# Block attention with a mixture of experts on one core: when the first weight parts are loaded and split

## Chip, core and metric

One NeuronCore of a Trainium2 chip runs the kernel; a core has five engines that run side by side, each its own list of instructions in order: TensorE (PE in the profile, its weight loads PEld), VectorE (DVE), ScalarE (ACT), GpSimd (POOL) and SyncE (SP), which here issues nearly all DMAs. The metric is the device time in microseconds (us), the median of several runs. Lower is better.

## What is computed

Attention over 4 batches, 8 heads, 576 positions and a head size of 64, where a position sees its own 64-block and all earlier ones; its output, laid out as a [2304, 512] matrix `x`, goes through four experts with weights `p`:

```python
attn = softmax(mask(q @ k.T / 8))          # mask: block_i >= block_j, blocks of 64
x = (attn @ v) as [B*S, H*D]               # [2304, 512]
p = domain_probs / (domain_probs.sum(-1, keepdims=True) + 1e-9)
for e in range(4):
    h = np.maximum(x @ w1[e], 0.0)         # [2304, 1024]
    out += p[:, e:e + 1] * (h @ w2[e])     # [2304, 512]
```

All is float32. A float32 product in the experts is made as three products of a fast format (`fp32r`): each operand is split into a high part (a CAST) and a low part (operand minus high part, a TENSOR_TENSOR), and high x high, low x high and high x low are added.

## The kernel before

**Blocks and chunks.** The 2304 rows of `x` are cut into five blocks (`BLOCKS`): the first has 256 rows, the first 64 positions of each batch, the other four 512 rows each. The experts' work on a block is cut into 32 chunks, (expert, 128 of the 1024 hidden columns). Chunk i has two steps on PE: `mm1` (L1009), 12 matmuls `h <- w1h/w1l, xh/xl` in four groups of three, one group for each quarter of the 512 columns of `x`; and `mm2` (L1051), `acc <- w2h/w2l, hh/hl`, three matmuls for each 128 rows of the block (two such tiles in the first block). Between them `relu` (L1037) makes `hh` on ACT and `hl` on DVE. `moe_thread` (L996) runs mm1(0), mm1(1), mm2(0), mm1(2), mm2(1) and so on.

**Weights.** Two threads, `w_thread(1)` for W1 and `w_thread(2)` for W2 (L945), go through the chunks. `w_load` (L938) takes one of three raw buffers (`w1r0` to `w1r2`, `w2r0` to `w2r2`) and issues a 256 KB DMA; `w_split` (L971) then has `halves` (L961) make the high part (CAST on ACT or DVE) and the low part (on DVE) into one of four buffers `w1h0` to `w1h3`, `w1l0` to `w1l3`, and the same for W2, and gives the raw buffer back.

**The first block's attention** (`first_block`, L801) runs before everything else, in four steps of two heads (`step`, L824; step c0 makes quarter c0 of `x`). A step transposes K and Q on PE (L840), multiplies them (L864), takes the row maximum on DVE (L879, L881), exponentials on ACT (L884), the division on DVE (L888 to L890, result in `o3`), transposes the result (L894, copied to `xs` on ACT), multiplies with V (L907), and splits the result into `xh` and `xl`. `left_first[0]` counts the steps that are still open: it is 4 at first and 0 when the last `xl` of the first block is recorded. While PE would be idle in this stage, `warm_up` (L364) puts in matmuls whose result nobody reads (L365).

**The attention of the other blocks** is cut into 16 units (`unit`, L390), each a batch and two heads; the K, Q and V of a unit are loaded into `kr`, `qr` and `VN` (L402, L436, L463), transposed on DVE into `kT` (L416) and `qT` (L450) once `left_first[0]` is 0, and multiplied on PE (L510 in the first four units). PE mixes this with the experts' work on blocks that are ready.

**What sets the order.** A recording layer (`Flow`, L77) runs all threads when the program is built. Each thread offers its next operation; the layer estimates when each could start, takes the earliest, and at equal times the lowest priority number (L182 to L185). So each engine's list of instructions is fixed when the kernel is built, and a thread that says `("until", condition)` offers nothing until the condition holds in the recording. `w_prio` (L934) gives the priority of a weight part's DMA and splits: as long as chunk 0 is current (`now[0] == 0`) it is 1.6 for chunk 0 and 2.005 for all later ones; the first unit's K and Q have 2.0, its V 2.005 (L470), the first block's loads 1.1 and its steps 1.2 to 1.23.

Of the kernel before, what the change touches and what calls it, by code (L numbers as in the profile page):

```python
# [211 lines left out]
def kernel(  # L212
# [131 lines left out]
    def a_copy(dst, src, n, r, u, prio=0.0, ps=False):  # L344
        engs = [("act", 0.833 * n + (55 if ps else 95)), ("dve", (1.04 if ps else 0.52) * n + 70)]
        o = op(engs, 0, lambda e: nc.scalar.copy(dst, src) if e == "act" else nc.vector.tensor_copy(dst, src), r, u, prio)  # L346
        o.port = not ps
        return o

    def tt(eng, dst, a, b, alu, n, r, u, prio=0.0):  # L350
        both = {"dve": 1.04 * n + 70, "pool": 2.1 * n + 365}
        engs = [(e, both[e]) for e in (eng if isinstance(eng, list) else [eng])]
        o = op(engs, 0, lambda e: ENG[e].tensor_tensor(out=dst, in0=a, in1=b, op=alu), r, u, prio)  # L353
        o.port = a.space != PSUM and b.space != PSUM
        return o
# [24 lines left out]
    now, loads = [0], [0]  # L380
    left_first = [len(STEPS)]
# [551 lines left out]

    def w_prio(i, which):  # L934
        i -= 4 * (i >= NC) * (which == 1)
        return lambda: (1.6 if i == 0 else 2.005) if now[0] == 0 else 1.0 if i <= now[0] + 1 else (2.5 if i <= now[0] + 2 else 5.0)

    def w_load(which, i, e, f):  # L938
        raw = yield fl.take(f"w{which}r")
# [18 lines left out]
    def flat(raw):  # L958
        return raw.tile.rearrange("p c f -> p (c f)") if len(raw.tile.shape) == 3 else raw.tile

    def halves(which, turn, src, n, deps, raw, pr, more=()):  # L961

        hi = yield fl.take(f"w{which}h", turn)
        lo = yield fl.take(f"w{which}l", turn)
        a = yield a_copy(hi.tile[:, :n], src, n, deps, [raw, hi], pr)
        o = tt(BOTH, lo.tile[:, :n], src, hi.tile[:, :n], SUB, n, deps + [a], [raw, hi, lo], pr)
        o.pen = lambda: 1000.0 if now[0] == 0 else 300.0
        l = yield o
        return hi, lo, a, l

    def w_split(which, i, raw, v0, pr):  # L971
        wt[i, which] = yield from halves(which, i, flat(raw), DM, [v0], raw, pr)
        fl.give(raw)

# [429 lines left out]
```

## Time and profile before

| | |
|---|---|
| median of 3 runs | 898.09 us (897.37 to 898.21) |
| the profiled execution's own time | 898.77 us |
| span of its trace, first to last instruction | 896.7 us |
| PE busy | 887.7 us, 99% of the span |
| DVE, ACT, POOL busy | 689.0, 455.7, 139.4 us |
| HBM read and written | 85.63 MB and 4.72 MB |

The trace is of one execution. 2.1 us of its 898.77 lie outside the span. An engine counts as busy while an instruction of it runs; ends of matmuls are modelled, so a busy PE is not a PE at its peak. The granted clock is the share of TensorE's full clock (2.4 GHz) that it was given; 0.50 is 1.2 GHz.

### The profile page before, as it was taken

To read this page: it belongs to the slowest core of one execution; us is meant where nothing else is said; L and a number is where in the kernel's file an instruction comes from. 1 tells how busy PE (TensorE), PEld (TensorE's weight loads), DVE (VectorE), ACT (ScalarE), POOL (GpSimd) and SP (SyncE) were. 2 spreads that over 40 slices of the span, in tenths; PEclk is the share of its full clock that TensorE was granted. 3 is DMA by queue.
4 is the path that set the end of the run, shared out by engine and by line. 5 is a ranking of instruction groups with operands and counts; after the bars stand their busy time and mean duration, and the time that the engine had idled before them with its cause. 6 is when DMAs were issued, how large, how long until landed. Compare 5 with 4: busy or idle time off the path is not lost.

```text
span 896.7 us, 12489 instructions
## 1 busy us (share of the span) xinstructions
PE 887.7 (99%) x4342; PEld 715.7 (80%) x4344; DVE 689.0 (77%) x1293; ACT 455.7 (51%) x886; POOL 139.4 (16%) x53
## 2 busy tenths in 40 slices
PE   8999999999999999999999999999999999999998
PEld 5677788877787887787787787888888888888886
DVE  6799998989888988997897787975565655666532
ACT  4687765656556556665555554655343333333220
POOL 1111000244312232414213413000000000000000
PEclk9999999999999999999999999999999999999999
DMA  7775547724553554454443233312120212110002
GB/s 173 187 205 153 160 130 183 202 84 110 122 145 73 127 122 120 144 133 110 112 114 96 74 104 96 127 60 60 36 71 30 77 36 71 47 48 24 12 1 94
DMA packets 212734, 91.17 MB, mean 102 GB/s; under 512 B 126400, under 2 KB 193984, under 8 KB 212672
## 3 DMA queue, kind: packets, MB, share of 16 engines
q1 hardware_dynamic: 210464, 89.59, 37.5%
q10 hardware_dynamic: 2208, 0.79, 0.4%
q8 instruction: 34, 0.56, 0.3%
q14 instruction: 28, 0.23, 0.1%
HBM read 85.63 MB, written 4.72 MB: 101 GB/s over the span
## 4 chain that ended last, share of the span: by engine, by line
PE 95%; DMA 2%; DVE 1%; ACT 1%; issue 0%; SPq 0%; DVEq 0%; ACTq 0%
PE h L1023 24%; PE acc L1074 24%; PE acc L1310 19%; PE h L1247 10%; PE att L1247 7%; PE att L734 5%; PE att L522 2%; PE att L523 2%; DMA w2r<-in_moe_w_dram 1%; PE acc L510 1%; DMA cm<-in_q_dram 1%; PE att L510 0%; PE acc L734 0%; SPq L340 0%; ACT o L884 0%
## 5 line engine op out<-in xcount | busy, mean ns | idle before, releaser
L1023 PE MATMUL h<-xl,w1h 128*128 128x512 f32 (+1 forms) x384 | 136.3, 355 | 2.0 <-DVE xl L353 1.8
L1023 PE MATMUL h<-xh,w1h 128*128 128x512 f32 (+1 forms) x384 | 137.7, 359 | 0.0
L1023 PE MATMUL h<-xh,w1l 128*128 128x512 f32 (+1 forms) x384 | 136.2, 355 | 0.0
L1074 PE MATMUL acc<-w2h,hh 128*128 128x512 f32 x312 | 123.4, 395 | 0.0
L1074 PE MATMUL acc<-w2l,hh 128*128 128x512 f32 x312 | 121.8, 390 | 0.0
L1074 PE MATMUL acc<-w2h,hl 128*128 128x512 f32 x312 | 121.6, 390 | 0.0
L346 ACT CAST w2h<-w2r 128x512 fp32r<-128x512 f32 x113 | 70.5, 623 | 71.1 <-PE acc L1074 56.3
L667 POOL PARTITION_ALL_REDUCE sb<-sa x24 | 78.4, 3315 | 137.5 <-DVE sa L353 92.3
L688 POOL PARTITION_ALL_REDUCE mx<-cm x16 | 56.9, 3554 | 268.1 <-DVE cm L353 211.6
L353 DVE TENSOR_TENSOR w1l<-w1r,w1h 128x512 fp32r<-128x512 f32 (+1 forms) x124 | 85.9, 693 | 0.6
L353 DVE TENSOR_TENSOR w2l<-w2r,w2h 128x512 fp32r<-128x512 f32 x116 | 80.6, 697 | 7.0 <-ACT w2h L346 6.7
L1041 ACT ACTIVATE hh<-h 128x512 fp32r<-128x512 f32 (+1 forms) x94 | 49.4, 526 | 67.2 <-PE h L1023 66.3
L1023 PEld LDWEIGHTS h<-xl,w1h 128*128 128x128 f32 x384 | 72.8, 190 | 12.6 <-DVE xl L353 2.4
L1023 PEld LDWEIGHTS h<-xh,w1h 128*128 128x128 f32 x384 | 72.7, 189 | 12.1 <-issue 1.7
L1023 PEld LDWEIGHTS h<-xh,w1l 128*128 128x128 f32 x384 | 72.7, 189 | 10.3
L346 ACT CAST w1h<-w1r 128x512 fp32r<-128x512 f32 x116 | 69.1, 598 | 14.2 <-PE att L1247 5.7
L1074 PEld LDWEIGHTS acc<-w2h,hh 128*128 128x128 f32 x312 | 58.8, 188 | 12.9 <-issue 2.1
L1074 PEld LDWEIGHTS acc<-w2h,hl 128*128 128x128 f32 x312 | 58.6, 188 | 12.8
L346 ACT COPY S<-att 128x512 f32<-128x512 f32 (+2 forms) x92 | 49.0, 532 | 36.5 <-DVE att L592 21.6
L1074 PEld LDWEIGHTS acc<-w2l,hh 128*128 128x128 f32 x312 | 58.8, 188 | 10.2
L353 DVE TENSOR_TENSOR S<-S,mx 128x1024 f32<-128x1024 f32 (+4 forms) x80 | 60.2, 789 | 3.2 <-POOL mx L688 3.2
L1043 DVE SCALAR_TENSOR_TENSOR hl<-h,hh 128x512 fp32r<-128x512 f32 (+1 forms) x94 | 55.2, 587 | 6.3 <-ACT hh L1041 6.0
(336 smaller groups left out, 1812.8 us busy)
## 6 DMA issues: line engine op xcount, KB each, us to landing
w2r<-in_moe_w_dram SPq DMA_DIRECT2D x128, 256.0 KB, 2.9
w1r<-in_moe_w_dram SPq DMA_DIRECT2D x120, 256.0 KB, 3.0
qr<-in_q_dram SPq DMA_DIRECT2D x112, 64.0 KB, 2.3
kr<-in_k_dram SPq DMA_DIRECT2D x64, 72.0 KB, 2.9
VN<-in_v_dram SPq DMA_DIRECT2D x32, 128.0 KB, 2.5
out_dram<-o SPq DMA_DIRECT2D x12, 256.0 KB, 2.1
w1rp<-in_moe_w_dram SPq DMA_DIRECT2D x8, 256.0 KB, 2.9
out_dram<-op SPq DMA_DIRECT2D x4, 256.0 KB, 2.1
```

Of the source, the lines that this page charges most:

```text
L346: o = op(engs, 0, lambda e: nc.scalar.copy(dst, src) if e == "act" else nc.vector.tensor_copy(dst, src), r, u, prio)
L353: o = op(engs, 0, lambda e: ENG[e].tensor_tensor(out=dst, in0=a, in1=b, op=alu), r, u, prio)
L522: nc.tensor.matmul(out=o, lhsT=KK.tile[:, at:at + n], rhs=Hv[:, hs, lo:W], start=True, stop=False)
L667: sums.append((yield op("pool", 150 + 6.3 * W, lambda _, h=h: nc.gpsimd.partition_all_reduce(sb.tile[:, h * W:h * W + W], sa.tile[:, h * W ...
L688: lambda _: nc.gpsimd.partition_all_reduce(mx.tile[:, :2 * W], src, P, RED.max),
L734: nc.tensor.matmul(out=x.tile[64 * g:64 * g + 64, W - w:W], lhsT=lhsT, rhs=rhs, start=(i == 0), stop=(i == len(todo) - 1))
L1023: nc.tensor.matmul(out=ps[:, :n], lhsT=s.tile[:, ks], rhs=x.tile[:, kc, :n], start=(kc == 0 and m == 0), stop=(kc == KC - 1 and m == 2),)
L1041: a = yield op("act", 0.833 * n + 55, lambda _: nc.scalar.activation(hh.tile[:, :n], ps[:, :n], AF.Relu), [mm], [pb, hh], 0.0)
L1043: l = yield op("dve", 1.04 * n + 70, lambda _: nc.vector.scalar_tensor_tensor(out=hl.tile[:, :n], in0=ps[:, :n], scalar=0.0, in1=hh.tile[: ...
L1074: nc.tensor.matmul(out=acc, lhsT=s.tile[:, ts], rhs=w.tile, start=(f == 0 and m == 0), stop=(f == FC - 1 and m == 2))
L1247: nc.tensor.matmul(out=ps[:, :n], lhsT=w.tile[:, ks], rhs=x[:, kc, :n], start=(start and kc == 0 and m == 0), stop=(i in (2, 3, 4) and kc ...
L1310: nc.tensor.matmul(out=acc, lhsT=s.tile[:, ts], rhs=w.tile, start=(c == 0 and x == 0), stop=(c == 3 and x == 2))
```

## The change

Two edits. The priority of the W1 part of chunk 1 (`i + which == 2` holds for i = 1 and which = 1 alone, since chunk 0 is named before) goes from 2.005 to 1.7 while chunk 0 is current, so that its DMA is recorded ahead of the first unit's K, Q and V. And every other weight part after chunk 0's two (`i + which > 2`: W2 of chunk 1, and all of chunk 2 and later) is not split before `left_first[0]` is 0, that is, before the last `xl` of the first block is recorded. The loads themselves are not held.

```diff
     def w_prio(i, which):
         i -= 4 * (i >= NC) * (which == 1)
-        return lambda: (1.6 if i == 0 else 2.005) if now[0] == 0 else 1.0 if i <= now[0] + 1 else (2.5 if i <= now[0] + 2 else 5.0)
+        return lambda: (1.6 if i == 0 else 1.7 if i + which == 2 else 2.005) if now[0] == 0 else 1.0 if i <= now[0] + 1 else (2.5 if i <= now[0] + 2 else 5.0)
...
     def w_split(which, i, raw, v0, pr):
+        if i + which > 2:
+            yield ("until", lambda: left_first[0] == 0)
         wt[i, which] = yield from halves(which, i, flat(raw), DM, [v0], raw, pr)
         fl.give(raw)
```

The recorded order changes from there on to the end of the program, on PE, DVE, ACT and SP. Lines after L973 stand two lines lower in the changed kernel (mm1's L1023 is L1025 there, mm2's L1074 is L1076, relu's L1043 is L1045). Three places follow. A row is line, operation, written buffer <- read buffers, shape.

**DVE, around the last `xl` of the first block.** Before, from the division of the last step (`o3_90`) to the first unit's `kT` (`xl0_93` is written once for each step; `w1h1`, `w1h3` and `w1l1` to `w1l3` are parts of chunks 1 to 3):

```order
L890 TENSOR_TENSOR o3_90<-o3_90,st3_98 128x256
L353 TENSOR_TENSOR xl0_93<-acc1_131,xh0_91 128x256
L346 CAST w1h1_62<-w1r1_78 128x512
L353 TENSOR_TENSOR w1l1_66<-w1r1_78,w1h1_62 128x512
L353 TENSOR_TENSOR xl0_93<-acc0_130,xh0_91 128x256
L353 TENSOR_TENSOR w1l2_67<-w1r2_79,w1h2_63 128x512
L346 CAST w1h3_64<-w1r0_77 128x512
L353 TENSOR_TENSOR w1l3_68<-w1r0_77,w1h3_64 128x512
L353 TENSOR_TENSOR xl0_93<-acc3_133,xh0_91 128x256
L416 STREAM_TRANSPOSE kT0_110<-kr0_107 128x576
```

With the change, first the rows from chunk 0's last low part to the last step's row maximum, where chunk 1's W1 now stands:

```order
L353 TENSOR_TENSOR w2l0_73<-w2r0_80,w2h0_69 128x512
L346 CAST w1h1_62<-w1r1_78 128x512
L879 TENSOR_REDUCE st3_98<-att0_134 128x4
L353 TENSOR_TENSOR w1l1_66<-w1r1_78,w1h1_62 128x512
L353 TENSOR_TENSOR xl0_93<-acc3_133,xh0_91 128x256
L888 TENSOR_SCALAR st2_97<-st2_97 128x4
L881 TENSOR_SCALAR st3_98<-st3_98 128x4
```

and then the rows from the last step's division to the first unit's `qT`:

```order
L890 TENSOR_TENSOR o3_90<-o3_90,st3_98 128x256
L353 TENSOR_TENSOR xl0_93<-acc2_132,xh0_91 128x256
L353 TENSOR_TENSOR xl0_93<-acc3_133,xh0_91 128x256
L416 STREAM_TRANSPOSE kT0_110<-kr0_107 128x576
L353 TENSOR_TENSOR w1l2_67<-w1r2_79,w1h2_63 128x512
L353 TENSOR_TENSOR w2l1_74<-w2r1_81,w2h1_70 128x512
L353 TENSOR_TENSOR w2l2_75<-w2r2_82,w2h2_71 128x512
L1045 SCALAR_TENSOR_TENSOR hl0_85<-h0_128,hh0_83 128x256
L450 STREAM_TRANSPOSE qT0_111<-qr0_109 128x512
```

The five weight instructions between the last `xl`s have gone. Two of them (chunk 1) stand ahead of the last step's row maximum; `w1l2`, `w2l1` and `w2l2` stand between the last `xl` and chunk 0's `hl0`, and `hl0` between them and `qT`.

**ACT, around chunk 0's `hh0`.** Before:

```order
L346 CAST w1h2_63<-w1r2_79 128x512
L346 CAST xh0_91<-acc3_133 128x256
L346 CAST w2h1_70<-w2r1_81 128x512
L1041 ACTIVATE hh0_83<-h0_128 128x256
L346 CAST w2h2_71<-w2r2_82 128x512
L346 CAST w2h3_72<-w2r0_80 128x512
```

With the change:

```order
L346 CAST xh0_91<-acc3_133 128x256
L346 CAST w1h2_63<-w1r2_79 128x512
L346 CAST w1h3_64<-w1r0_77 128x512
L346 CAST w2h1_70<-w2r1_81 128x512
L346 CAST w2h2_71<-w2r2_82 128x512
L1043 ACTIVATE hh0_83<-h0_128 128x256
```

The last step's `xh` no longer stands behind a weight cast; four weight casts stand between it and `hh0` where one stood. On PE the recorded order after mm1(1) is now the first three matmuls of mm2(0) (`hh0`, `hh0`, `hl0`) and then the first unit's L510; before, it was L510 and then all six of mm2(0).

**SP, around the third load into `w1r2`** (W1 of chunk 5). Before, from the second unit's V (`VN1`) to the third unit's K (`kr0`):

```order
L340 DMA VN1_117<-in_v_dram 128x4x64
L340 DMA probs_n_102<-in_moe_domain_probs_dram 64x4
L340 DMA w1r1_78<-in_moe_w1_dram 128x4x128
L340 DMA probs_n_102<-in_moe_domain_probs_dram 64x4 x2
L340 DMA w1r2_79<-in_moe_w1_dram 128x4x128
L340 DMA probs_n_102<-in_moe_domain_probs_dram 64x4
L340 DMA w1r0_77<-in_moe_w1_dram 128x4x128
L340 DMA kr0_107<-in_k_dram 32x18x32 x3
```

With the change:

```order
L340 DMA VN1_117<-in_v_dram 128x4x64
L340 DMA probs_n_102<-in_moe_domain_probs_dram 64x4 x4
L340 DMA kr0_107<-in_k_dram 32x18x32 x4
L340 DMA w1r2_79<-in_moe_w1_dram 128x4x128
L340 DMA qr0_109<-in_q_dram 32x16x32 x4
L340 DMA w1r0_77<-in_moe_w1_dram 128x4x128
```

On ACT the instruction that waits for that load stands right ahead of chunk 2's `hh0`:

```order
L557 ACTIVATE att1_135<-ident_101 64x2x64
L346 CAST w1h1_62<-w1r2_79 128x512
L1043 ACTIVATE hh0_83<-h0_128 128x256
```

The third load into `w1r1` has gone up to behind the first of the second unit's four K loads; the one into `w1r2` has gone down behind all four K loads of the third unit. On ACT the same three rows stood there before.

## Rows read from the trace of the kernel before

**Rows 1.** Page: span, and busy time of each engine (share), instructions.

```profile
span 896.7 us, 12489 instructions
PE 887.7 (99%) x4342; PEld 715.7 (80%) x4344; DVE 689.0 (77%) x1293; ACT 455.7 (51%) x886; POOL 139.4 (16%) x53
```

**Rows 2.** Windows: length, busy PE, PEld, DVE, ACT, POOL; granted clock; DMA share, GB/s.

```profile
26.30:29.70 3.40, 3.40 (x14) 2.15 (x14) 2.63 (x6) 1.40 (x3) 0.00 (x0) 0.50 0.54 112
45.00:145.00 100.00, 100.00 (x630) 79.37 (x630) 94.65 (x178) 72.88 (x157) 10.27 (x3) 1.00 0.59 166
145.00:560.00 415.00, 415.00 (x1970) 332.19 (x1969) 362.30 (x689) 234.47 (x435) 121.78 (x36) 1.00 0.46 117
```

**Rows 3.** Timeline of PE: start, us, instruction, count, [idle before <- releaser].

```profile
23.10 0.33 PE L1023 MATMUL h<-xh,w1h 128*128 128x256 f32 x1
25.27 0.39 PE L1023 MATMUL h<-xl,w1h 128*128 128x256 f32 x1 [1.84 <-DVE xl L353]
25.49 0.28 PE L1023 MATMUL h<-xh,w1l 128*128 128x256 f32 x1
25.60 0.28 PE L1023 MATMUL h<-xh,w1h 128*128 128x256 f32 x1
...
27.42 0.41 PE L1023 MATMUL h<-xh,w1l 128*128 128x256 f32 x1
27.76 2.07 PE L510 MATMUL att<-qT,kT 64*128 64x512 f32 x4
...
30.68 0.50 PE L1074 MATMUL acc<-w2h,hh 128*128 128x512 f32 x1
...
34.84 0.40 PE L1074 MATMUL acc<-w2h,hh 128*128 128x512 f32 x1
...
37.66 0.40 PE L1074 MATMUL acc<-w2h,hh 128*128 128x512 f32 x1
```

**Rows 4.** Timeline of DVE, same columns.

```profile
16.58 0.16 DVE L881 TENSOR_SCALAR st<-st 128x4 f32<-128x4 f32 x1
...
18.79 0.42 DVE L890 TENSOR_TENSOR o<-o,st 128x256 f32<-128x256 f32 x1
...
22.75 0.69 DVE L353 TENSOR_TENSOR w1l<-w1r,w1h 128x512 fp32r<-128x512 f32 x1
23.72 0.43 DVE L346 CAST w1h<-w1r 128x512 fp32r<-128x512 f32 x1 [0.28 <-DMA w1r<-in_moe_w_dram]
24.18 0.69 DVE L353 TENSOR_TENSOR w1l<-w1r,w1h 128x512 fp32r<-128x512 f32 x1
24.79 0.42 DVE L353 TENSOR_TENSOR xl<-acc,xh 128x256 fp32r<-128x256 f32 x1
...
26.39 0.70 DVE L450 STREAM_TRANSPOSE qT<-qr 128x512 f32<-128x512 f32 x1
27.01 0.39 DVE L1043 SCALAR_TENSOR_TENSOR hl<-h,hh 128x256 fp32r<-128x256 f32 x1
```

**Rows 5.** Timeline of ACT, same columns.

```profile
20.80 0.38 ACT L346 COPY xs<-acc 128x256 f32<-128x256 f32 x1
22.10 0.62 ACT L346 CAST w1h<-w1r 128x512 fp32r<-128x512 f32 x1 [0.92 <-DMA w1r<-in_moe_w_dram]
22.62 0.37 ACT L346 CAST xh<-acc 128x256 fp32r<-128x256 f32 x1
25.02 0.62 ACT L346 CAST w2h<-w2r 128x512 fp32r<-128x512 f32 x1 [2.03 <-DMA w2r<-in_moe_w_dram]
...
26.09 1.27 ACT L346 CAST w2h<-w2r 128x512 fp32r<-128x512 f32 x2
```

**Rows 6.** SP's issues, and the landing times of the `w1r` loads, 27 to 36 us.

```profile
30.53 0.53 SPq L340 DMA_DIRECT2D w1r<-in_moe_w_dram x1
...
32.35 2.56 SPq L340 DMA_DIRECT2D kr<-in_k_dram x3
...
DMA to landing us min/median/max: 3.0/3.0/3.9
```

## The prediction

> **What bounds the kernel now.** I read the page's busy times first: PE is busy for 887.7 of 896.7 us [rows 1], so time can come only from stretches in which PE idles or runs at a low clock. The windows say where these are: from 45 to 560 us PE is busy for all 515 us, and DVE beside it for 94.65 of the first 100 [rows 2]; what is changed there can cost time, not win any. The window from 26.30 to 29.70 has a granted clock of 0.50, which is 1.2 GHz instead of 2.4 [rows 2]. The timeline of PE shows what came before the clock fell: one idle stretch of 1.84 us, which ended at 25.27 when an `xl` was there [rows 3]. The timeline of DVE shows why that `xl`, the first block's last, was late: it started at 24.79, behind a `w1l` (22.75), a weight cast that waited for its DMA (23.72) and another `w1l` (24.18) [rows 4], none of which it needs. Its own input, `xh`, was done at 22.62 + 0.37 = 22.99 [rows 5].
>
> So the stretch to win back is 1.84 us of idle time plus half of 3.4 us at half the clock, 1.7: 3.5 us, 0.4% of the time. A measurement of this kernel can tell about 0.2%, 1.8 us.
>
> The sum is made on the profiled execution, 898.77 us, of which the span is 896.7; the median of the runs is 898.09, 0.68 below. I apply the difference to the median.
>
> **Step 1, the last `xl`.** Five weight instructions leave DVE's list ahead of it, and one cast leaves ACT's list ahead of `xh`. From `xs` (20.80) by `xh` (22.62) and `xl` to PE, the step's own chain is then 22.62 + 0.37 + 0.42 and about 0.1 of handing over: PE would go on at 23.5. But chunk 1's cast and `w1l` now stand ahead of the last step's L881 (16.58, and through it L890 at 18.79 [rows 4]): 0.43 + 0.69 = 1.1 us by the rows of the same kind at 23.72 and 24.18. All of it on the path would make 24.6. On PE the step's transpose stands behind the step before anyway, which hides part of it; I take 0.4, nearer to the low end, and 23.9. The raw part itself is now issued ahead of the first unit's loads; if it landed after 15.9, where DVE reaches its cast, the same chain would be later by that much, but step 2 shows that the first microsecond of this costs nothing. The K, Q and V of the first unit are issued one transfer later and are not needed before the last `xl`, whose wait they were not part of [rows 3].
>
> After 23.9, 14 matmuls at 0.11 to 0.12 each (25.49 to 25.60 [rows 3]) end mm1(1) at 25.55; before, the last of them was issued at 27.42, half of them at half the clock, and the next work came at 27.76. Ahead by 2.1 us.
>
> **Step 2, what is late next: `hh0`.** PE's next work is now mm2(0), which needs chunk 0's `hh0`. On ACT that stands behind four weight casts instead of one. The rows bound when these can run: W2 of chunk 1 was there at 25.02, where ACT had waited 2.03 us for it, and W2 of chunk 2 by 26.09 [rows 5]. So the fourth cast starts between 25.6 and 26.1, and `hh0` is done between 26.5 and 27.0. I take 26.9, near the rows: the loads that stand ahead of these are the same as before, only in another order. Were all of them up to 0.9 earlier (chunk 2's W1 was at 22.10 the second of its row and would be the first), `hh0` would be done at 26.0. PE waits 1.35 us (0.45 to 1.45). The third matmul needs `hl0`, which DVE makes after `w2l2` (0.69) and in 0.39 [rows 4]: 27.65, 0.3 after the two `hh0` matmuls. L510 needs `qT`, 0.70 behind `hl0` [rows 4]: 28.3, 0.4 after the third. Together 2.05 us of idle time where before L510 simply followed.
>
> [...]
>
> **Step 3, to chunk 2.** From L510's start to the end of mm1(2) it took 34.84 − 27.76 = 7.08 us [rows 3]. Now three of the six mm2(0) matmuls are done before (0.23 each: 2.82 us from 34.84 to 37.66 hold six of them and 12 of 0.12), 0.69 less, and if the clock holds, half of the 1.94 us to 29.70 is saved, 0.97. 28.3 + 5.42 = 33.7: ahead by 1.1 us.
>
> **Step 4, `w1r2`'s third load.** Before mm2(2), ACT's `hh0` of chunk 2 stands behind the cast of chunk 5's W1, and that load has moved behind four K loads on SP. It was issued at 30.53, and a `w1r` load here landed 3.0 (median) to 3.9 us after its issue [rows 6]. Now one more W1 load (0.53) and four K loads stand ahead, at 0.45 each if the queue is free and 0.85 if it is as in the row (2.56 for three [rows 6]): issued at 32.9 to 34.5, landed at 35.9 to 38.4. Below that, the W1 loads that no longer stand between could free up to another 0.8: 35.1. I take 35.9, since no big transfer now stands between the small ones. `hh0` then ends 0.62 + 0.38 later at 36.9 and `hl0` 0.62 + 0.69 + 0.39 later at 37.6. PE comes to mm2(2) at 37.66 − 1.1 = 36.55 and waits 0.35 and 0.25: ahead by 0.5 us that remain.
>
> **Step 5, the rest.** PE's work is the same matmuls; the order differs in a few changes of kind. At equal work and a full PE the 0.5 us stay to the end. Sum: 898.09 − 0.5 = **897.6 us**, with 896.5 to 898.8 for this case.
>
> **Rivals.**
> - *The transfers come early enough.* Chunk 2's and chunk 5's loads land at the low bounds of steps 2 and 4 (26.0 for `hh0`, 35.1 for `w1r2`). Step 2 then costs 1.1 instead of 2.05, and step 4 0.3 or nothing: ahead by 1.8 to 2.1, 896.0 us. With no wait at all it would be 3.5, 894.6. For it: a load's time to landing varies by 0.9 [rows 6]. Against: it takes both.
> - *`w1r2` decides, slower.* Each microsecond that this load lands after 36.4 is lost one for one, since PE can't pass it and mm2(2) ends with it. At 37.5 it is +1.1, at the upper bound of 38.4 +2.0: 899.2 to 900.1 us, I take 899.4. For it: three K loads took 2.56 us of SP's queue [rows 6].
> - *The clock falls again.* One idle stretch of 1.84 us was followed by 3.4 us at 1.2 GHz [rows 2, 3]; now 2.05 us of idle time lie between 25.55 and 28.3, in three parts. If the clock falls, 1.7 us go: 1.1 ahead becomes 0.6 behind, and step 4's wait is covered: 898.7 us.
> - *A later wait.* DVE has 5% to spare from 45 to 145 us [rows 2], and all of its list is reordered there; two or three weight parts late by one DVE instruction (0.69) each would cost about 2 us: 899.9 us. Before, PE waited nowhere in that stretch.
>
> That the change does nothing is excluded by the rows of the order: the five instructions have gone.
>
> **Chances and numbers.** My case 0.42; early transfers 0.20; late `w1r2` 0.15; the clock 0.13; a later wait 0.10. Faster by over 0.2% (below 896.3) are most of the early transfers, 0.18. Slower by over 0.2% (above 899.9) are the top of the late `w1r2` and of the clock and half of the later wait, 0.12. Within: 0.70. The range leaves one in ten on either side: 895.8 to 899.9.
>
> **What would show it.** Step 1 is right if PE's wait for the last `xl` is under 0.6 us and ends between 23.5 and 24.6; step 2 if PE then waits 0.5 to 1.5 us for ACT's `hh0` at about 26.9, with ACT's wait for the W2 DMA just before it; step 4 if a second wait for `hh0` ends near 37 with ACT waiting for a `w1r` DMA. A granted clock of 1.00 up to 45 us belongs to my case, 0.50 in a window from about 26 to 32 to the rival of the clock. The prediction is wrong if PE does not wait for `hh0` at all, or if waits of more than half a microsecond stand after 45 us.

## The result: 5.3 us slower, and the profile after

| | before | after |
|---|---|---|
| median of the runs, us | 898.15 (897.37 to 898.83, 4 runs) | 903.42 (902.73 to 904.67, 4 runs) |
| profiled execution, us | 898.77 | 903.55 |
| span of it, us | 896.7 | 901.4 |

The ratio is 1.0058, with a 95% interval of 1.0044 to 1.0072. Forecast was 897.6 us in a range of 895.8 to 899.9; the time lies 3.5 us above the range.

The page of the changed kernel, span and busy times, which answers to [rows 1]:

```profile
span 901.4 us, 12519 instructions
PE 889.5 (99%) x4347; PEld 715.3 (79%) x4347; DVE 696.2 (77%) x1290; ACT 454.6 (50%) x889; POOL 139.8 (16%) x53
```

The windows, with the columns of [rows 2]:

```profile
26.30:29.70 3.40, 2.54 (x9) 1.17 (x11) 3.31 (x7) 2.21 (x6) 0.00 (x0) 1.00 0.61 121
29.70:34.00 4.30, 4.30 (x32) 3.32 (x29) 0.74 (x2) 3.51 (x12) 0.00 (x0) 1.00 0.21 37
...
39.68:43.09 3.41, 3.41 (x11) 2.55 (x11) 3.14 (x9) 2.24 (x6) 0.00 (x0) 0.50 0.94 240
45.00:145.00 100.00, 99.64 (x629) 78.48 (x626) 92.53 (x173) 72.66 (x161) 11.70 (x4) 1.00 0.60 159
145.00:560.00 415.00, 414.18 (x1970) 331.17 (x1969) 369.27 (x685) 233.93 (x440) 122.50 (x36) 1.00 0.47 118
```

The first window had a granted clock of 0.50 before and has 1.00 now; the 3.4 us at 0.50 have not gone, they stand at 39.68. At 0.50 PE's matmuls of 512 columns begin 0.427 us apart (from 40.78 to 42.06), 1.2 columns a ns; at 1.00 the fastest of 512 columns, the warm-up's, begin 0.216 us apart (at 15.67), 2.4 columns a ns. These two paces are what the prediction calls 1.2 and 2.4 GHz. In the window from 29.70 to 34.00 the DMA engines are busy for 0.21 of the time and move 37 GB/s, and DVE does 0.74 us of work in 4.3; it stands there for the probabilities:

```profile
34.11 0.16 DVE L1332 TENSOR_REDUCE probs_s<-probs_n 128x2 f32<-128x8 f32 x1 [3.67 <-DMA probs_n<-in_moe_domain_probs_dram]
```

That window is the exception. Over the stretch in which the loads are late, and in its first part, the same columns say:

```profile
19.60:26.60 7.00, 5.80 (x43) 4.79 (x41) 3.12 (x6) 3.24 (x8) 0.00 (x0) 1.00 0.99 262
...
19.60:50.20 30.60, 26.25 (x156) 19.70 (x154) 20.34 (x42) 16.57 (x43) 3.52 (x1) 0.94 0.78 179
```

The DMA engines are busy for 0.78 of the stretch (0.79 before), and for 0.99 of its first 7 us.

The timeline of PE, which answers to [rows 3] (the lines of this kernel are two higher):

```profile
23.59 0.39 PE L1025 MATMUL h<-xl,w1h 128*128 128x256 f32 x1
...
27.00 0.50 PE L1076 MATMUL acc<-w2h,hh 128*128 128x512 f32 x1 [1.47 <-ACT hh L1043]
...
27.77 0.49 PE L1076 MATMUL acc<-w2h,hl 128*128 128x512 f32 x1
28.39 0.70 PE L510 MATMUL att<-qT,kT 64*128 64x512 f32 x2
...
33.84 0.40 PE L1076 MATMUL acc<-w2h,hh 128*128 128x512 f32 x1
...
36.54 0.28 PE L1025 MATMUL h<-xh,w1l 128*128 128x256 f32 x1
39.41 0.59 PE L1076 MATMUL acc<-w2h,hh 128*128 128x512 f32 x1 [2.59 <-ACT hh L1043]
```

PE goes on with the last `xl` at 23.59 without a wait to speak of, waits 1.47 us for chunk 0's `hh`, and is 1.0 us ahead of before at 33.84 (34.84 in [rows 3]). Then it stands for 2.6 us for chunk 2's `hh`, and the clock falls behind that. The timeline of ACT says what `hh` was waiting for:

```profile
38.46 0.62 ACT L346 CAST w1h<-w1r 128x512 fp32r<-128x512 f32 x1 [5.11 <-DMA w1r<-in_moe_w_dram]
38.98 0.38 ACT L1043 ACTIVATE hh<-h 128x256 fp32r<-128x256 f32 x1
...
41.01 0.62 ACT L346 CAST w1h<-w1r 128x512 fp32r<-128x512 f32 x1 [1.17 <-DMA w1r<-in_moe_w_dram]
```

ACT had stood for 5.1 us with the cast of chunk 5's W1 at the head of its list. And the issues of SP (start, us that the issues took, what, how many) say why that load was late; they answer to [rows 6]:

```profile
26.66 2.10 SPq L340 DMA_DIRECT2D VN<-in_v_dram  x4
28.81 2.43 SPq L340 DMA_DIRECT2D probs_n<-in_moe_domain_probs_dram  x4
31.34 3.42 SPq L340 DMA_DIRECT2D kr<-in_k_dram  x4
34.86 0.44 SPq L340 DMA_DIRECT2D w1r<-in_moe_w_dram  x1
```

The load was issued at 34.86 instead of 30.53 and used at 38.46, 3.6 us later. No row has an idle time: SP goes from one issue to the next. From 19.3 to 50.2 us it makes 49 issues, whose rows take 29.6 of these 30.9 us; before, 49 took 29.5 of the 31.5 us from 19.1 to 50.6. Most issues take 0.4 to 0.6 us each. A few are longer, and one of these is in the row of four K loads, whose other three took 0.50 each:

```profile
31.34 1.80 SPq L340 DMA_DIRECT2D kr<-in_k_dram  x1
```

Beside it stands one packet of the queue that carries instructions (packets, MB, share of 16 engines, from 31.2 to 33.2 us):

```profile
q8 instruction: 1, 0.02, 4.5%
```

By the trace's DMA records it has 16 KB and lasts from 31.33 to 32.78; the issue ends 0.37 later. In all 14 traces one issue between SP's 42nd and 47th takes 1.0 to 2.0 us, whatever it loads (a 1 KB load of the probabilities 1.86 in `after_w1_first`, a W1 load 1.49 in `w1_before_k`). Before, it ends at 34.37, 0.41 us after such a packet (32.99 to 33.96). That SP stands for this packet is read from the agreement of these two; no run moved the packet. Before, the load into `w1r2` was issued 2.3 us ahead of that issue (30.53 and 32.85); now it stands behind it. Of the 4.3 us by which it is issued later, 1.3 are the excess of this one issue.

The waits of PE for other engines that are new since before (in us: total, times, longest):

```profile
PE acc L1076 <- ACT hh L1043: 4.1, 2, 2.6
...
PE att L734 <- DVE cm L353: 0.6, 1, 0.6
...
PE att L510 <- ACT cm L346: 0.4, 1, 0.4
PE att L571 <- DVE cm L353: 0.2, 1, 0.2
```

So the 4.7 us of span are: 1.0 won by 33.84; 2.75 lost before mm2 of chunk 2 (from 36.54 to 39.41, less one matmul of 0.12); half of 3.41, 1.7, lost to the clock (the eleven matmuls from 39.41 to 43.12 took 3.71 us, the same kinds from 33.84 to 35.82 at a clock of 1.00 took 1.98); that makes 3.45 behind, and chunk 12's first matmul is 3.54 behind (76.64 instead of 73.10). From there to about 355 us nothing is added for good; about 1.2 us are lost in the order of the rest, 0.8 of them in waits of PE at 410 and 422 us.

### The profile page after: what moved, and what is told of

The parts are those of the page before. It is cut to its first block, busy times and chain, and to the rows that moved or that the text cites. A ratio compares the mean times of both kernels' runs of the same rounds, so it can differ in the third digit from the quotient of the medians.

```text
span 901.4 us, 12519 instructions
## 1 busy us (share of the span) xinstructions
PE 889.5 (99%) x4347; PEld 715.3 (79%) x4347; DVE 696.2 (77%) x1290; ACT 454.6 (50%) x889; POOL 139.8 (16%) x53
## 4 chain that ended last, share of the span: by engine, by line
PE 91%; DMA 2%; DVE 2%; SPq 2%; ACT 1%; issue 1%; POOL 0%; DVEq 0%; POOLq 0%; ACTq 0%
PE acc L1076 22%; PE h L1025 22%; PE acc L1312 19%; PE h L1249 10%; PE att L1249 7%; PE att L734 4%; PE att L522 2%; SPq L340 2%; PE att L523 2%; DMA w1r<-in_moe_w_dram 1%; PE acc L734 1%; PE acc L510 1%; DMA cm<-in_q_dram 1%; DMA probs_n<-in_moe_domain_probs_dram 0%; POOL mx L688 0%
## 5 line engine op out<-in xcount | busy, mean ns | idle before, releaser
L1025 PE MATMUL h<-xh,w1h 128*128 128x512 f32 (+1 forms) x384 | 138.1, 360 | 0.1
L1025 PE MATMUL h<-xl,w1h 128*128 128x512 f32 (+1 forms) x384 | 136.1, 354 | 0.1
L1025 PE MATMUL h<-xh,w1l 128*128 128x512 f32 (+1 forms) x384 | 136.1, 354 | 0.0
L1076 PE MATMUL acc<-w2h,hh 128*128 128x512 f32 x312 | 123.7, 397 | 4.1 <-ACT hh L1043 4.1
L1076 PE MATMUL acc<-w2h,hl 128*128 128x512 f32 x312 | 122.3, 392 | 0.0
L1076 PE MATMUL acc<-w2l,hh 128*128 128x512 f32 x312 | 122.3, 392 | 0.0
L667 POOL PARTITION_ALL_REDUCE sb<-sa x24 | 80.7, 3409 | 144.1 <-DVE sa L353 86.7
L688 POOL PARTITION_ALL_REDUCE mx<-cm x16 | 55.0, 3438 | 261.3 <-DVE cm L353 202.4
L353 DVE TENSOR_TENSOR w1l<-w1r,w1h 128x512 fp32r<-128x512 f32 (+1 forms) x128 | 89.7, 700 | 3.3 <-ACT w1h L346 2.5
L353 DVE TENSOR_TENSOR w2l<-w2r,w2h 128x512 fp32r<-128x512 f32 x116 | 84.2, 727 | 7.9 <-ACT w2h L346 7.6
L346 ACT CAST w1h<-w1r 128x512 fp32r<-128x512 f32 (+1 forms) x116 | 70.6, 613 | 29.5 <-DMA w1r<-in_moe_w_dram 11.8
L1043 ACT ACTIVATE hh<-h 128x512 fp32r<-128x512 f32 (+1 forms) x94 | 49.2, 523 | 68.0 <-PE h L1025 67.9
L1025 PEld LDWEIGHTS h<-xh,w1h 128*128 128x128 f32 x384 | 72.8, 189 | 13.3 <-issue 2.5
L1025 PEld LDWEIGHTS h<-xl,w1h 128*128 128x128 f32 x384 | 72.8, 190 | 10.5 <-DVE xl L353 0.3
L1025 PEld LDWEIGHTS h<-xh,w1l 128*128 128x128 f32 x384 | 72.6, 189 | 10.3
L1076 PEld LDWEIGHTS acc<-w2h,hh 128*128 128x128 f32 x312 | 58.9, 189 | 16.4 <-ACT hh L1043 4.5
L1076 PEld LDWEIGHTS acc<-w2h,hl 128*128 128x128 f32 x312 | 58.8, 189 | 13.7 <-DVE hl L1045 1.0
L346 ACT COPY S<-att 128x512 f32<-128x512 f32 (+2 forms) x96 | 51.2, 533 | 32.1 <-DVE att L592 21.3
L1076 PEld LDWEIGHTS acc<-w2l,hh 128*128 128x128 f32 x312 | 58.9, 189 | 10.1
L1045 DVE SCALAR_TENSOR_TENSOR hl<-h,hh 128x512 fp32r<-128x512 f32 (+1 forms) x94 | 55.1, 586 | 6.4 <-ACT hh L1043 6.2
```

Of the source, the lines that this page charges most:

```text
L667: sums.append((yield op("pool", 150 + 6.3 * W, lambda _, h=h: nc.gpsimd.partition_all_reduce(sb.tile[:, h * W:h * W + W], sa.tile[:, h * W ...
L688: lambda _: nc.gpsimd.partition_all_reduce(mx.tile[:, :2 * W], src, P, RED.max),
L1025: nc.tensor.matmul(out=ps[:, :n], lhsT=s.tile[:, ks], rhs=x.tile[:, kc, :n], start=(kc == 0 and m == 0), stop=(kc == KC - 1 and m == 2),)
L1043: a = yield op("act", 0.833 * n + 55, lambda _: nc.scalar.activation(hh.tile[:, :n], ps[:, :n], AF.Relu), [mm], [pb, hh], 0.0)
L1045: l = yield op("dve", 1.04 * n + 70, lambda _: nc.vector.scalar_tensor_tensor(out=hl.tile[:, :n], in0=ps[:, :n], scalar=0.0, in1=hh.tile[: ...
L1076: nc.tensor.matmul(out=acc, lhsT=s.tile[:, ts], rhs=w.tile, start=(f == 0 and m == 0), stop=(f == FC - 1 and m == 2))
```

## The experiments

Twelve kernels. Each was timed beside the kernel before, whose medians were 898.3 to 898.7 in these series.

### First series: which order makes the wait

The theory after reading the trace (A): ACT's `hh` behind a late load is the loss, and the clock that follows it. To test it the order of ACT was turned round (`relu_first`), the order of SP (`w1_before_k`), and the two parts of the change were made alone.

`relu_first` splits the W1 parts of chunks 5 to 7 behind the `hh` of chunks 2 to 4:

```diff
     def w_split(which, i, raw, v0, pr):
         if i + which > 2:
             yield ("until", lambda: left_first[0] == 0)
+        if which == 1 and 5 <= i <= 7:
+            yield ("until", lambda: hts.get(i - 3) is not None)
```

> The change with one more rule: the second-to-next W1 parts of chunks 5, 6 and 7 are split only after hh of chunks 2, 3 and 4 is recorded. The transfers keep the order of the change up to 40 us, so chunk 5's W1 should again be issued at about 34.9 and land at about 38.4; only ACT's hh of chunk 2 now stands ahead of the cast of that load. Theory A (the loss is ACT's hh standing behind a late load, and the clock that fell after PE had stood for it): PE's 2.6 us wait for hh at 39.4 goes, the clock stays at 1.00 from 29 to 45 us, and with these 2.75 + 1.71 us gone the time is 899.0 (898.3 to 899.7), about 1 above or equal to before since 1.2 us of later waits stay. Rival B (the clock falls anyway, from the idle time between 25.5 and 28.4): the wait goes, but 3.4 us at 1.2 GHz appear somewhere before 45: 900.7. Rival C (the loss sits in the reordered rest after 45 us, and a wait won is given back there): 902.5 or more.

Measured: 903.66 us (902.23 to 904.60), the same as the change. PE's wait for chunk 2's `hh` went. In its place PE waited for `qT`, and DVE's transpose waited for the third unit's Q (a line of PE's timeline and one of DVE's):

```profile
39.84 1.93 PE L510 MATMUL acc<-qT,kT 64*128 64x512 f32 x4 [1.66 <-DVE qT L450]
```
```profile
39.08 0.71 DVE L450 STREAM_TRANSPOSE qT<-qr 128x512 f32<-128x512 f32 x1 [2.48 <-DMA qr<-in_q_dram]
```

From 40.04 to 43.45 the granted clock was 0.50 again. Theory A is right in the wait that it names and wrong in its price: the next load in SP's queue was late too. Rival C has the time, and the place in part: at chunk 15 this kernel is 1.80 us behind the kernel before, where the change is 3.54, and after 355 us it loses another 1.9 where the change loses 1.2.

`w1_before_k` holds the third unit's K back until chunk 5's W1 is issued:

```diff
+    issued = [0]
...
         def k_thread():
             yield ("until", lambda: now[0] >= gate[u])
             yield ("until", lambda: started())
+            yield ("until", lambda: u != 2 or issued[0] > 5)
...
         v0 = yield dma(raw.tile, src, P * DM * 4, u=[raw], prio=pr)
+        issued[0] += which == 1
```

> The change with one more rule: the third unit's K loads wait until chunk 5's W1 is issued, so that on SP this load stands ahead of four K loads instead of behind them; ACT's order is as in the change, hh of chunk 2 still behind the cast of that load. Theory A (the four K issues, 3.4 us of SP's queue, made the load late): it is issued at about 31.4 instead of 34.9 and lands at 34.5 to 35.5, PE waits for hh of chunk 2 by less than 0.5 us, the clock stays at 1.00: 899.0 (898.3 to 900). Rival B (the transfers themselves are slow there, whatever the order of issue, as behind the four probs loads): it lands at 36.5 or later, a wait of 1 us or more stays, and if the clock falls behind it the time is 901 to 903. Rival C (the loss sits after 45 us): 902.5 or more.

Measured: 901.08 us (899.86 to 901.53), 2.3 less than the change. The load was issued at 30.45 and its cast began at 34.45; PE waited 0.6 us for `hh` and the clock stayed at 1.00. Then PE waited 0.4 us, until 42.0, for a `cm` of DVE and 1.2, until 47.7, for one of ACT. Between theory A and rival C.

`hold_only` keeps the hold and undoes the early load of chunk 1's W1 (its expectation calls the hold the first part of the change, and the next one the early load the second):

```diff
-        return lambda: (1.6 if i == 0 else 1.7 if i + which == 2 else 2.005) if now[0] == 0 else 1.0 if i <= now[0] + 1 else (2.5 if i <= now[0] + 2 else 5.0)
+        return lambda: (1.6 if i == 0 else 2.005) if now[0] == 0 else 1.0 if i <= now[0] + 1 else (2.5 if i <= now[0] + 2 else 5.0)
```

and `load_only` keeps the early load and undoes the hold:

```diff
     def w_split(which, i, raw, v0, pr):
-        if i + which > 2:
-            yield ("until", lambda: left_first[0] == 0)
```

> The first part of the change alone: weight parts of later chunks held until the first block's last x; raw W1 of chunk 1 stays behind the first unit's K, Q and V as before. On ACT one cast fewer stands ahead of chunk 0's hh and chunk 2's hh stands ahead of the cast of chunk 5's W1, though on SP that load now stands even behind the third unit's K and Q. Theory A: the last x goes through at about 23.6 as in the change; PE waits for chunk 0's hh until 26.5 to 27 with 1 us or less; no wait for chunk 2's hh, no fall of the clock to 45 us: mm2(2) begins 1 to 1.5 us earlier than before, so 897.0 (896.0 to 898.5) if nothing is lost later, 898.2 with the same 1.2 us of later waits. Rival B (holding the weight parts by itself makes the load late and that is the loss, whatever stands on ACT): a wait of 2 us or more before mm2(2) and 902 to 904. Rival C (clock falls at the first waits): 898.7 to 900.

Measured: 901.37 us (900.60 to 902.47). No fall of the clock, but PE waited 1.5 us for an `hl` until 37.4, 0.4 until 41.9, 0.9 for an `hh` until 52.1 and 1.0 until 414.6. None of the three numbers came true. Rival B is nearest: the first of these waits stands in mm2(2). It is for chunk 2's `hl`, not its `hh`, and the late load behind it is not a weight: DVE had stood with the probabilities at the head of its list, and was busy from there to `hl`.

```profile
33.82 0.16 DVE L1332 TENSOR_REDUCE probs_s<-probs_n 128x2 f32<-128x8 f32 x1 [5.21 <-DMA probs_n<-in_moe_domain_probs_dram]
```

> The second part of the change alone: raw W1 of chunk 1 ahead of the first unit's K, Q and V, weight parts not held. On SP chunk 5's W1 stands between the probs loads, ahead of the third unit's K; on ACT chunk 0's hh stands behind two weight casts and chunk 2's hh behind the cast of chunk 5's W1, as in the change; on DVE the last xl but one stands behind a weight cast and its low part again. Theory A (late load): no wait at mm2(2), the first idle stretch of before is partly there (0.5 to 1.8 us, and the clock may fall after it, 1.7): 896.5 to 898.5, I take 897.5. Rival B (the early load itself costs, by what it moves on ACT: hh of chunk 2 behind the cast): a wait at mm2(2) of 1 us or more: 900 or more. Rival C (the loss sits after 45 us, from any reordering): 899.5 or more with no wait over 0.5 us before 45.

Measured: 907.88 us (905.53 to 909.19), the slowest. Its longest waits on PE:

```profile
PE att L522 <- DVE cm L353: 3.5, 2, 2.9
PE h L1023 <- DVE xl L353: 2.0, 2, 1.2
PE acc L510 <- ACT cm L346: 2.0, 1, 2.0
```

The wait for `xl` is there as before (the part alone does not free it), the 2.0 for `cm` end at 47.1 and the 2.9 at about 396, and behind each of these two the clock was at 0.50 for 3.4 us. Rival C has the time here, though not its condition of no long wait before 45 us; and one move early in the program brought a 2.9 us wait 350 us later.

What the four have in common: SP issued without a pause from 20 to 40 us (not to 50, as the next expectation says: `hold_only` pauses for 1.2 us at 40.7, `relu_first` and `w1_before_k` for 1.8 and 2.0 near 49), and whatever wait was taken away, another came before 50 us. Theory S: SP's queue of issues is the limit in this stretch. Rival D: the transfers themselves are. Rival O: any new order brings new waits, since the recorder sets the lists of all engines from modelled times, and the lists do not fit the chip's.

### Second series: fewer issues in the full stretch

The eight small loads of the probabilities (1 to 2 KB each) and the V loads of the first two units (first used at about 60 us) stand in the full stretch. What DVE makes of the probabilities is first used at 57 us, but its work on the first four loads stands in its list much earlier, at 34.11 in the change; the expectations, which say 60 us, leave that out. They were held back, in the changed kernel and, as a control, in the kernel before.

`probs_late`, on the change, and `before_probs_late`, on the kernel before:

```diff
-            yield ("until", lambda: now[0] >= 32 * (min(bi, PAIR) - 1) and started())
+            yield ("until", lambda: now[0] >= (2, 16, 32)[min(bi, 2)] and started())
```

`after_small_late` and `before_small_late` have (3, 16, 32) there, and hold the V loads too:

```diff
         def v_thread():
-            yield ("until", lambda: now[0] >= gate[u])
+            yield ("until", lambda: now[0] >= (4 if u < 2 else gate[u]))
```

> The change with the eight small loads of the router's probabilities taken out of SP's queue between 28.8 and 41 us (the first four wait for chunk 2, the next four for chunk 16; they are first used at about 60 us). ACT keeps the order of the change, hh of chunk 2 behind the cast of chunk 5's W1. In the four runs so far SP issued without a pause from 20 to 50 us. Theory S (SP's queue of issues is the limit in that stretch, and a load comes as late as the issues ahead of it take): chunk 5's W1 is issued 2.4 us earlier, at 32.4, lands at about 36, PE waits for hh of chunk 2 by at most 0.7 us, the clock stays at 1.00 to 45 us, DVE's 3.7 us wait for the probabilities goes: 899.4 (898.3 to 900.5). Rival D (the transfers themselves, not their issue, are the limit): the load lands at 37.5 or later, a wait of 1.5 us or more stays: 901.5 to 903.5. Rival O (any new order of this stretch makes some instruction wait, since the recorded order no longer fits the times of the chip): the wait for hh goes and another of 1 us or more comes: 901 or more.

Measured: 901.38 us (901.01 to 902.40). SP's issue of the load, and the cast on ACT:

```profile
29.81 0.44 SPq L340 DMA_DIRECT2D w1r<-in_moe_w_dram  x1
```
```profile
33.71 0.62 ACT L346 CAST w1h<-w1r 128x512 fp32r<-128x512 f32 x1 [1.79 <-DMA w1r<-in_moe_w_dram]
```

The load came 4.7 us earlier than in the change, the wait for `hh` and the fall of the clock went, and at chunk 9 PE was 1.0 us ahead of the kernel before (56.43 against 57.41) and 3.6 ahead of the change. Theory S is right up to there, and rival D is not: four loads of 1 KB are next to no bytes. The 4.7 us are more than the 2.4 that S expected; one more reason is that the long issue (1.6 us, at 30.35, of a Q load) now came behind this load and not ahead of it. Then 0.8 us went at 71.6 (L510 for `cm`) and 1.6 at 247.2 (L522 for `cm`), the first at twice its size in the change, the second in a place where neither kernel waits: rival O.

> The control: the kernel before with the same eight small loads held back. Theory S: before, PE waits for no load between 28 and 50 us, so nothing is won there, and the 1.8 us wait for the last xl and the 3.4 us at 1.2 GHz after it stay: 898.2 (897.4 to 899). Rival O: a new wait of 1 us or more: 899.5 or more. Rival D: as theory S.

Measured: 902.62 us (900.63 to 902.96), as rival O said. The wait for the last `xl` grew from 1.8 to 2.5 us, and L522 waited 1.3 us at 218.

> The change with both the probabilities (until chunk 3) and the V loads of the first two units (until chunk 4; first used at 61 us) taken out of the full stretch of SP's queue, 12 issues of about 0.55 us or 6.6 us before chunk 5's W1. Theory S: chunk 5's W1 is issued at about 28, as soon as its buffer is free, and lands before 33; the wait for chunk 0's hh at 27.0 shrinks from 1.5 to under 1 us since W2 of chunks 1 and 2 comes earlier; no wait of 0.7 us or more from 28 to 50 us and no fall of the clock: the 3.5 us of the stretch before are won but for 1 to 1.5: 895.8 (894.8 to 897.3). Rival O: waits of 2 us or more in sum before 60 us: 898.5 or more. Rival D: between, 898 to 900.

Measured: 907.36 us (906.53 to 909.72). At chunk 9 this kernel is 2.7 us ahead of before (54.70 against 57.41). Then PE waited 1.1 us, until 60.96, for DVE, in whose list the work on the probabilities now stood, and the clock fell at 63.1; at 581.76, in the second half of the program, came

```profile
581.76 0.69 PE L1249 MATMUL att<-S4l,w1h 128*128 128x512 f32 x1 [3.43 <-DVE S4l L353]
```

with another 3.4 us at 0.50 behind it. Theory S for the first 55 us, rival O for the rest.

> The kernel before with the same twelve loads held back, without the change. Theory S: the weight work that stands ahead of the last xl on DVE no longer waits for its load (0.4 to 0.9 us), but two weight parts and a cast more stand there, so PE's wait for the last xl stays between 1 and 3 us, with the fall of the clock after it; nothing else waits: 898 (896.5 to 899.5), so that the change is worth about 2 us once SP's queue is free. Rival O: 900 or more.

Measured: 907.04 us (906.47 to 907.99), with the same wait of 3.4 us near 580: rival O for the whole. But PE's wait for the last `xl` was 0.6 us, the clock did not fall behind it, and at chunk 8 this kernel was 3.7 us ahead of before (50.90 against 54.59), more than theory S had said for it. In the times of whole programs these four runs confound the two theories, since holding an issue back changes the lists of every engine to the end of the program.

### Third series: SP's order alone

Here the recorder decides as it did; a few loads are only written down later. PE, ACT, DVE and POOL get word for word the lists of the kernel that is altered.

```diff
+            if op.later and self.sent < N:
+                self.held.append((op.fn, eng))
+            else:
                 op.fn(eng)
+                self.sent += eng == "sp"
+                while self.held and self.sent >= N:
+                    fn, e = self.held.pop(0)
+                    fn(e)
```

`after_w1_first` has N = 44 and marks the four K loads of the third unit as later; `after_v_queue`, `before_v_queue` and `hold_v_queue` (which is `hold_only` with it) have N = 67 and mark the eight V loads of units 0 and 1.

> The change with one swap on SP alone: chunk 5's W1 load is issued ahead of the third unit's four K loads instead of behind them. PE, ACT, DVE and POOL run the change's instructions in the change's order, word for word. Theory S (the place in SP's queue made the load late): issued at 31.4, landed by 35, chunk 2's hh at about 35.6, so PE's wait of 2.6 us for it and the fall of the clock behind it go. The third unit's Q lands no earlier than in the change, about 39.8, so PE may wait up to 1.2 us for qT at about 40.5, as in the run with hh first. 899 to 900.5, I take 900.0, with the change's later waits of 1.2 us as they are; 901.7 if the clock falls behind the wait for qT. Rival D (the load is slow whenever it is issued there): landed at 37 or later, 901.5 or more. Rival O (a wait won returns in full): 902.5 or more.

Measured: 903.70 us (902.26 to 904.77). The wait for chunk 2's `hh` fell from 2.6 to 0.4 us and the clock stayed at 1.00, so the place in SP's queue did make that wait. But ACT then stood with the cast of the next W1 load, and the `S` copies of the third unit behind it; its timeline and PE's:

```profile
40.55 0.62 ACT L356 CAST w1h<-w1r 128x512 fp32r<-128x512 f32 x1 [4.05 <-DMA w1r<-in_moe_w_dram]
41.08 0.58 ACT L356 COPY S<-att 128x512 f32<-128x512 f32 x1
```
```profile
43.04 0.99 PE L520 MATMUL att<-qT,kT 64*128 64x448 f32 x4 [1.60 <-ACT w2h L356]
```

That cast began at 41.01 in the change: the load came when it came, whatever PE had won. The swap within the full queue moved the wait to the next load. (At chunk 13 this execution is 1.1 us ahead of the change's. It then lost 2.4 us between 170 and 225 us, in waits that the change with the same order did not have; this is left open, and this execution is the slowest of the six.)

> The change with only SP's order altered in another way: the eight V loads of the first two units, which stand ahead of W1 and W2 of chunks 1 to 3 and of the third unit's loads, go behind the loads of the 49th microsecond, where SP is out of work until 55; they are first used at 61 us. All other engines run the change's instructions in the change's order, word for word. Theory S: every load from 17 to 45 us comes 2 to 4.4 us earlier: chunk 0's hh at 26.3 or before instead of 27.0, no wait for chunk 2's hh nor for qT, no fall of the clock, PE about 2 us ahead of the kernel before at 45 us. With the change's later waits of 1.2 us 897.7 (896.8 to 899). Rival O: 900 or more. If waits after 45 us grow as PE comes earlier (DVE is busy for 93% of the time there), up to 2 us of it go: 899.7.

Measured: 899.00 us (897.59 to 899.33), 4.4 less than the change, and the same as the kernel before (ratio 0.9999, 0.9990 to 1.0008). SP, ACT and PE:

```profile
29.57 0.44 SPq L349 DMA_DIRECT2D w1r<-in_moe_w_dram  x1
```
```profile
34.31 0.62 ACT L356 CAST w1h<-w1r 128x512 fp32r<-128x512 f32 x1 [1.98 <-DMA w1r<-in_moe_w_dram]
```
```profile
35.65 0.40 PE L1086 MATMUL acc<-w2h,hh 128*128 128x512 f32 x1
```

PE comes to mm2 of chunk 2 without a wait, and no clock below 1.00 is granted until the last few microseconds. The time lies at the upper end of theory S's range (896.8 to 899). The lists are those of the change, so no new order is in it. The eight V loads are 640 KB, though, so this run alone does not part issues from bytes.

> The control: the kernel before with the same eight V loads moved on SP alone, the other engines word for word as before. Theory S: nothing but the weight work ahead of the last xl is waiting for loads here; the cast at 23.72 waited 0.28 us, so the last xl is 0.3 us earlier, and the fall of the clock stays: 897.8 (897 to 898.5). Should the first stretch be freed by more (PE's wait under 1 us and no fall of the clock): 895.5. Rival O: 899.5 or more.

Measured: 894.87 us (894.66 to 895.66), ratio 0.9956 (0.9943 to 0.9969): 3.9 us faster than the kernel before, 8.6 below the change's 903.42, and the version to take. The forecast of 897.8 won far too little; the case for which the expectation names 895.5, a first stretch freed by more, is what came. Its page, the window in which the clock had fallen, and the one wait of PE in the stretch:

```profile
span 892.9 us, 12491 instructions
PE 885.1 (99%) x4344; PEld 713.9 (80%) x4344; DVE 688.7 (77%) x1293; ACT 456.0 (51%) x886; POOL 139.3 (16%) x53
```
```profile
26.30:29.70 3.40, 3.40 (x24) 2.20 (x22) 1.17 (x4) 2.75 (x10) 0.00 (x0) 1.00 0.60 159
```
```profile
23.80 0.39 PE L1033 MATMUL h<-xl,w1h 128*128 128x256 f32 x1 [0.56 <-DVE xl L363]
```

The same weight instructions stand ahead of the last `xl` on DVE, but they wait less for their loads. The first of them, before and here:

```profile
21.22 0.43 DVE L346 CAST w1h<-w1r 128x512 fp32r<-128x512 f32 x1 [1.67 <-DMA w1r<-in_moe_w_dram]
```
```profile
19.81 0.43 DVE L356 CAST w1h<-w1r 128x512 fp32r<-128x512 f32 x1 [0.35 <-DMA w1r<-in_moe_w_dram]
```

The cast at 23.72 [rows 4] no longer waits at all. The three W1 loads behind these were issued from 17.63 on before and from 16.17 here, and landed 3.6, 3.9 and 4.6 us after their issue before and 3.6, 3.9 and 4.2 here: they come earlier because they are issued earlier, and hardly because the transfers are faster. So the 1.84 us of [rows 3] become 0.56 and the clock does not fall. Chunk 9 is 3.84 us ahead (53.57 against 57.41), chunk 95 again 3.84: with the lists unchanged nothing is given back.

> The hold alone (without the early W1), with the same eight V loads moved on SP and nothing else, the other engines word for word as in the run of the hold alone. Theory S: its waits before 55 us (1.5 for hl, 0.9 for hh, 0.4 for cm in that run) go with the late loads, the wait of 1.0 at 413 us for cm, which the recorded order made, stays: 898.0 (897 to 899.2), which is 3 more than the kernel before with the same loads moved, since there no later wait stood. If the hold by itself is worth something once SP's queue is free, 894.5 or less.

Measured: 897.42 us (896.28 to 898.52). This is in theory S's range (897 to 899.2). At chunk 9 it is 0.3 us ahead of `before_v_queue` (53.25), so the hold is worth little once the queue is free; by chunk 95 it is 1.5 behind. The later wait is the same in the two kernels that have this order, at 414.59 in `hold_only` and at 408.65 here:

```profile
414.59 0.42 PE L522 MATMUL att<-HH,KK 128*128 128x320 f32 x1 [1.02 <-DVE cm L353]
```
```profile
408.65 0.42 PE L532 MATMUL att<-HH,KK 128*128 128x320 f32 x1 [1.02 <-DVE cm L363]
```

and so is that of the change, in the change and in `after_v_queue`:

```profile
410.94 2.81 PE L734 MATMUL att<-S,VN 128*64 128x512 f32 x20 [0.58 <-DVE cm L353]
```
```profile
406.37 2.81 PE L744 MATMUL att<-S,VN 128*64 128x512 f32 x20 [0.68 <-DVE cm L363]
```

They move by 5.9 and 4.6 us with everything ahead of them and keep their size or nearly so: these waits belong to the recorded order, not to the time at which PE comes.

## Why the prediction was wrong, step by step

- **What bounds the kernel.** It said that the stretch to win back was 3.5 us, and its cause the weight instructions ahead of the last `xl` on DVE. The size was right. The cause was half: the instructions ahead cost what they do because their loads were late (DVE had stood 1.67 us for the first of them, until 21.22), and they were late because SP's queue was full. SP's rows were read for one load [rows 6] and not as a busy time. `before_v_queue` wins the whole 3.5 with DVE's list untouched.
- **Step 1**, the last `xl`: right. PE goes on at 23.59 (said 23.9, 23.5 to 24.6).
- **Step 2**, `hh0`: right. A wait of 1.47 until 27.00 (said 1.35 until 26.9), the third matmul at 27.77 (27.65), L510 at 28.39 (28.3).
- **Step 3**: right. 33.84 (said 33.7) at a clock of 1.00.
- **Step 4** failed, in the size of one term: the issues ahead of chunk 5's W1. "I take 35.9, since no big transfer now stands between the small ones" prices the four K loads at 0.45 us each and the landing at 3.0. The four took 3.42 us instead of 1.8, the load was issued at 34.86 instead of 32.9, and it was used 3.6 us later, at 38.46; the upper bound was 38.4. That sentence supposes that the size of transfers sets the pace. What counted here was SP's time for each issue, and it did not go by bytes: the probabilities took 2.43 us for four loads of 1 KB, a W1 load of 256 KB took 0.44, and the DMA engines were busy for 0.21 of the time from 29.70 to 34.00. And the row that stood there, 2.56 us for three K loads, was read as an even 0.85 each. It holds two of 0.45 and 0.49 and one long issue:

```profile
32.85 1.52 SPq L340 DMA_DIRECT2D kr<-in_k_dram  x1
```

  The load had stood ahead of that issue and moved behind it. The wait was 2.75 us instead of 0.60.
- **The clock.** The rival looked for it at 25.55 to 28.3, where about 2 us of idle time in three parts did not bring it down. It fell behind step 4's wait, and the rivals "late `w1r2`" and "the clock" were priced apart, as if only one could come: 898.15 − 1.0 + 2.75 + 1.7 = 901.6. Here the first came with the second behind it, and the range left that out.
- **Step 5**, "the 0.5 us stay to the end", failed by 1.2 us: that is part of "a later wait", at about half the price said (2 us). The wait of 0.58 us that ends at 410.94 is one of the signs of being wrong that the prediction names.
- Sum of the terms as measured: 901.6 + 1.2 = 902.8, against 903.4.

A single issue is short beside its load: 0.44 us on SP, and 3.6 from the issue until the load is used. Summed over the queue the short times are not small: 49 issues fill 29.6 of 30.9 us, in a stretch over which the DMA engines are busy for 0.78.

What stays open: from 19.6 to 26.6 us the DMA engines were as full as SP's queue (0.99), and two issues there took 2.61 and 1.06 us; that fewer bytes would have helped there was not tried apart from fewer issues. And with the V loads out of the way in both, the change is still 4.1 us slower than the kernel before (899.00 against 894.87). Some 2.75 of these stand at chunk 12 (72.01 against 69.26), in waits of 0.5 us and less and in a first matmul of chunk 0 that is 0.5 later; 1.3 come after 355 us. Which of the reordered instructions makes each of the small ones was not tried.

## What to carry to other kernels

Sum the issues of each DMA queue over the stretch as you sum an engine's busy time: here a queue that issued without a pause (29.6 of 30.9 us) made a load late even while the DMA engines were busy for 0.21 of the time (29.70 to 34.00), and the load that moved behind small ones was issued 4.3 us later, by the time of their issues and not by their bytes. Take a merged row of issues apart before you price one of them: a single long one made over half of it in both kernels (1.52 of 2.56 us before, 1.80 of 3.42 in the change). Swapping two loads in the full queue (`after_w1_first`, 903.70 us), or holding the work behind one (`relu_first`, 903.66), moved the wait to the next load; taking loads that are used much later out of the stretch removed it (`after_v_queue`, 899.00) or made it smaller (`before_v_queue`, 1.84 to 0.56 us and 894.87). Where a recorder sets all lists from a model of the times, change one queue with the other lists held fixed, or waits far down the program (3.43 us at 581.76 in `after_small_late`) will hide what the edit did.

## What was not expected of the hardware

- A load of 1 KB held SP for as long as one of 256 KB: 2.43 us for four of the first, 0.44 for one of the second, in rows close to each other.
- One issue between SP's 42nd and 47th took 1.0 to 2.0 us in every trace, between 29.7 and 34.7 us, and ended 0.41 us (before) and 0.37 us (the change) after a 16 KB packet of the instruction queue. Loads in flight over it landed late as well: in the change the third and fourth load of the probabilities 3.8 and 3.3 us after their issue, the first two after 2.2 and 2.1.
- The granted clock was 0.50 for 3.4 us after single idle stretches of PE of 1.66 (`relu_first`), 1.84 (before), 1.95 and 2.90 (`load_only`), 2.49 (`before_probs_late`), 2.59 (the change), 3.42 (`before_small_late`) and 3.43 us (`after_small_late`), and stayed at 1.00 after 1.47 (the change), 1.52 (`hold_only`) and 1.60 us (`after_w1_first`). It fell 0.2 us after PE went on in `relu_first` (40.04 behind 39.84), 0.3 in the change (39.68 behind 39.41), 1.0 before (26.28 behind 25.27) and 1.2 in `load_only` (48.34 behind 47.10). By half of 3.4 us each fall is put at about 1.7; in the change the eleven matmuls from 39.41 took 1.73 us longer than the same kinds at 1.00. The fall at 63.1 in `after_small_late` came 2 us behind a wait of only 1.07, so the length of the last wait alone does not tell it.
